# Chunk attention into a phase MLP: token mix with tokens on the output partitions, transposes as four 64x64 tiles, q and k in 512-byte runs, and an order written out

## Chip, cores and metric

The kernel runs on one core of a Trainium2 chip. The metric is the device time of one execution in microseconds (us), the median of several runs. A profile of one execution is read beside it.

## What is computed

The inputs q, k and v are float32 of shape (8, 8, 576, 64): batch, heads, tokens, head size. Attention works inside chunks of 64 tokens; its result x has 576 tokens of 512 channels for each batch element. A phase layer follows, with a mix over all tokens, and a last product with a ReLU.

```python
scores = (q_c @ k_c.T) / 8                 # for every batch element, head and chunk of 64 tokens
x = softmax(scores) @ v_c                  # x: (8, 576, 512), heads side by side
theta = x @ w_theta                        # 512 x 512
zr, zi = x * cos(theta), x * sin(theta)
y = w_tok_r @ zr + w_tok_i @ zi            # 576 x 576 each, over the tokens
u = x + y
out = u + max(u @ w_ch, 0)                 # 512 x 512, float32
```

## The kernel before

Batch elements are taken in four pairs. A pair has 1152 tokens, which make nine tiles of 128 tokens (NT = 9). Tiles 0 to 3 belong to the first element of the pair, tiles 5 to 8 to the second, and the middle tile 4 (MID) holds the last 64 tokens of the first and the first 64 tokens of the second. GROUPS puts the nine tiles into five groups: four of two tiles and the middle tile alone.

Each stage is a function that works on one group or tile of a pair `p`.

- `load_qk` (L108) and `load_v` (L116) load a tile of q, k or v through the GpSimd queue (POOL), which turns float32 into float16. Each read is a run of 64 float32, so 256 bytes. A tile's q and k lie in a buffer of the pool `nat`.
- `a1` (L176) transposes q and k of a group on TensorE (PE) with 128x128 tiles, and VectorE (DVE) copies the result out of PSUM (L183). `a2` (L198) makes the scores, with 64x64 tiles of the array, and ScalarE (ACT) takes the exponential (L205). `a3` (L223) multiplies by v; v has a column of ones, so the sum of the softmax comes with it, and VectorE divides (L230, L231).
- `a4` (L245) transposes x, and ScalarE copies it (L250). `a5` (L261) makes theta with 512-column matmuls, ScalarE takes the cosine and the sine (L271, L275), and VectorE makes zr and zi. In the middle tile, zr of one element and zi of the other are moved to the other half of the partitions by two SyncE (SP) DMAs from a buffer `zmid`, so that one array pass can take both parts of the token sum.
- `tok_w` (L144) transposes the token weights, held in `wnat`. It does this twice, once in the token order of each element of a pair, into `wT[0]` and `wT[1]`.
- `y` (L312) mixes tokens. It puts channels on the output partitions and tokens on the free axis: for each element and each of four channel blocks, nine pairs of 288-column matmuls are summed. VectorE adds x (L320), which gives uT, already transposed for the last product.
- `w` (L332) multiplies a tile of uT by w_ch. With four more matmuls against an identity (L339) it brings u back to token order. ScalarE takes the ReLU (L345), VectorE adds (L347), and SP stores the tile (L349).

PSUM is one pool of four buffers of two banks each; every stage takes its buffer from it. All the loads of the next pair are issued by `load_pair` when a pair starts. The function `weave` mixes two lists of steps, for instance the token mix of pair `p` with the attention of pair `p+1`; the order inside the engines is then set by the tile scheduler. Weight loads stand between those of the first pair: w_theta and the token weights after the middle tile, w_ch at the end.

Of the kernel before, what the change touches and what calls it, by code (L numbers as in the profile page):

```python
# [9 lines left out]
FP32 = mybir.dt.float32  # L10
# [5 lines left out]
def weave(main, filler):  # L16

    n, m = len(main), len(filler)
    done = 0
    for i, step in enumerate(main):  # L20
        step()
        want = ((i + 1) * m) // n
        while done < want:
            filler[done]()
            done += 1
# [3 lines left out]
def kernel(  # L29
# [14 lines left out]
    CH = 64  # L44
# [4 lines left out]
    T = 2 * S  # L49
    NT = T // P  # L50
    HS = S // 2
    KT = S // P
    scale = 1.0 / math.sqrt(D)
    MID = NT // 2


    GROUPS = [(0, 2), (2, 2), (4, 1), (5, 2), (7, 2)]
    VP = D + 2

    const = ctx.enter_context(tc.tile_pool(name="const", bufs=1))  # L60
    glob = ctx.enter_context(tc.tile_pool(name="glob", bufs=1))
    psum = ctx.enter_context(
        tc.tile_pool(name="psum", bufs=4, space=bass.MemoryType.PSUM)
    )
    nat = ctx.enter_context(tc.tile_pool(name="nat", bufs=6))
    qkp = ctx.enter_context(tc.tile_pool(name="qkp", bufs=3))
    epool = ctx.enter_context(tc.tile_pool(name="epool", bufs=6))
    pairp = ctx.enter_context(tc.tile_pool(name="pairp", bufs=2))
    trig = ctx.enter_context(tc.tile_pool(name="trig", bufs=3))
    outp = ctx.enter_context(tc.tile_pool(name="outp", bufs=4))  # L70


    id16 = const.tile([P, P], FP16, name="id16")
    make_identity(nc, id16)
    pihalf = const.tile([P, 1], FP32, name="pihalf")
    nc.vector.memset(pihalf, math.pi / 2.0)

    wtheta16 = glob.tile([P, NDB, DM], FP16, name="wtheta16")
    wch16 = glob.tile([P, NDB, DM], FP16, name="wch16")


    wT = [glob.tile([P, 2 * KT + 1, S], FP16, name=f"wT{i}") for i in range(2)]
    wnat = glob.tile([P, KT + 1, 2, S], FP16, name="wnat")
    NV = 2 * NT
    v16 = glob.tile([P, NV, H, VP], FP16, name="v16")
    nc.gpsimd.memset(v16[:, :, :, D : D + 1], 1.0)

    def psum2(name, dtype=FP32):
        n = 1024 if dtype == FP32 else 2048
        return psum.tile([P, n], dtype, name=name, tag="ps")  # L90

# [3 lines left out]
    def tok_ranges(j):  # L95

        if j < MID:
            return [(0, 0, j * P, P)]
        if j > MID:
            return [(0, 1, j * P - S, P)]  # L100
        return [(0, 0, MID * P, CH), (CH, 1, 0, CH)]

    def load_qk(p, j):
        t = nat.tile([P, 2, H, D], FP16, name="qk16")
        nats[p, j] = t
        for ti, ap in enumerate((q, k)):
            for pp, bb, s0, n in tok_ranges(j):
                nc.gpsimd.dma_start(  # L108
                    t[pp : pp + n, ti],
                    ap[2 * p + bb, :, s0 : s0 + n, :].rearrange("h s d -> s h d"),  # L110
                )

    def load_v(p, j):
        slot = (p % 2) * NT + j
        for pp, bb, s0, n in tok_ranges(j):
            nc.gpsimd.dma_start(  # L116
                v16[pp : pp + n, slot, :, 0:D],
                v[2 * p + bb, :, s0 : s0 + n, :].rearrange("h s d -> s h d"),
            )

    def load_tok_w():
        for ri, ap in enumerate((moe_w_tok_r, moe_w_tok_i)):
            nc.gpsimd.dma_start(
                wnat[:, 0:KT, ri, :],
                ap[0 : KT * P, :].rearrange("(a p) s -> p a s", p=P),
            )
            nc.gpsimd.dma_start(wnat[0:CH, KT, ri, :], ap[KT * P : S, :])
# [5 lines left out]
    def tok_w(par, kt):  # L133
        ps = psum2("ps_wT", FP16)
        for tb in range(KT + 1):
            nt = P if tb < KT else CH
            if kt < 2 * KT:
                s0 = (kt % KT) * P + (CH if par else 0)
                parts = [(slice(0, P), kt // KT, s0)]
            else:  # L140
                s0 = 0 if par else KT * P
                parts = [(slice(ri * CH, ri * CH + CH), ri, s0) for ri in range(2)]
            for rows, ri, s0 in parts:
                nc.tensor.transpose(  # L144
                    ps[rows, tb * P : tb * P + nt],
                    wnat[0:nt, tb, ri, s0 : s0 + rows.stop - rows.start],
                    id16[0:nt, 0:nt],
                )
        if kt % 2:
            nc.vector.tensor_copy(out=wT[par][:, kt, :], in_=ps[:, 0:S])  # L150
        else:
            nc.scalar.copy(out=wT[par][:, kt, :], in_=ps[:, 0:S])


    st = {}

    def new_pair(p):
        st[p] = dict(
            x=pairp.tile([P, NT, DM], FP16, name="x16", bufs=1),
            xT=pairp.tile([P, NDB, T], FP16, name="xT"),  # L160
            zr=pairp.tile([P, NT, DM], FP16, name="zr16"),
            zi=pairp.tile([P, NT, DM], FP16, name="zi16"),
            qkT={},
            eT={},
        )

    def a1(p, g):

        j0, n = GROUPS[g]
        ps = psum2("ps_qkT", FP16)  # L170
        psv = ps.rearrange("p (w e s) -> p w e s", w=2, e=NE)
        for jj in range(n):
            t = nats.pop((p, j0 + jj))
            for w in range(2):
                for e in range(NE):
                    nc.tensor.transpose(  # L176
                        psv[:, w, e, jj * P : jj * P + P],
                        t[:, w, 2 * e : 2 * e + 2, :].rearrange("s h d -> s (h d)"),
                        id16,
                    )  # L180
        qkT = qkp.tile([P, 2, NE, 2 * P], FP16, name="qkT")
        st[p]["qkT"][g] = qkT
        nc.vector.tensor_copy(  # L183
            out=qkT[:, :, :, 0 : n * P], in_=psv[:, :, :, 0 : n * P]
        )

    def a2(p, g):

        j0, n = GROUPS[g]
        qkT = st[p]["qkT"].pop(g)  # L190
        ps = psum2("ps_sT")
        psv = ps.rearrange("p (r j e c) -> p r j e c", r=2, j=2, e=NE)
        for jj in range(n):
            for e in range(NE):
                for par in range(2):
                    for cp in range(2):
                        sl = slice(jj * P + cp * CH, jj * P + cp * CH + CH)
                        nc.tensor.matmul(  # L198
                            psv[cp * CH : cp * CH + CH, par, jj, e, :],
                            qkT[par * D : par * D + D, 1, e, sl],  # L200
                            qkT[par * D : par * D + D, 0, e, sl],
                        )
        eT = epool.tile([P, 2, NE, 2, CH], FP16, name="eT")
        st[p]["eT"][g] = eT
        nc.scalar.activation(  # L205
            out=eT[:, 0:n].rearrange("p j e r c -> p r (j e) c"),
            in_=psv[:, :, 0:n].rearrange("p r j e c -> p r (j e) c"),
            func=AF.Exp,
            scale=scale,
        )  # L210

    def a3(p, j, g):

        j0, n = GROUPS[g]
        eT = st[p]["eT"][g]
        slot = (p % 2) * NT + j
        ps = psum2("ps_x")
        psv = ps.rearrange("p (f c) -> p f c", f=2)
        for h in range(H):
            hf, h4 = h // NE, h % NE  # L220
            for cp in range(2):
                sl = slice(cp * CH, cp * CH + CH)
                nc.tensor.matmul(  # L223
                    psv[sl, hf, h4 * (D + 1) : (h4 + 1) * (D + 1)],
                    eT[sl, j - j0, h // 2, h % 2, :],
                    v16[sl, slot, h, 0 : D + 1],
                )
        px = psv[:, :, 0 : NE * (D + 1)].rearrange("p f (h c) -> p f h c", h=NE)
        recip = trig.tile([P, 2, NE, 1], FP32, name="recip")
        nc.vector.reciprocal(out=recip, in_=px[:, :, :, D : D + 1])  # L230
        nc.vector.tensor_tensor(  # L231
            out=st[p]["x"][:, j, :].rearrange("s (f h d) -> s f h d", f=2, h=NE),
            in0=px[:, :, :, 0:D],
            in1=recip.broadcast_to((P, 2, NE, D)),
            op=ALU.mult,
        )

    def a4(p, g):

        j0, n = GROUPS[g]  # L240
        ps = psum2("ps_xT", FP16)
        psv = ps[:, 0 : NDB * n * P].rearrange("p (a s) -> p a s", a=NDB)
        for jj in range(n):
            for db in range(NDB):
                nc.tensor.transpose(  # L245
                    psv[:, db, jj * P : jj * P + P],
                    st[p]["x"][:, j0 + jj, db * P : db * P + P],
                    id16,
                )
        nc.scalar.copy(  # L250
            out=st[p]["xT"][:, :, j0 * P : (j0 + n) * P], in_=psv
        )

    def a5(p, g):

        j0, n = GROUPS[g]
        ps = psum2("ps_theta")
# [94 lines left out]
    def c(f, *a):  # L352
        return lambda: f(*a)
# [100 lines left out]
```

The softmax here doesn't subtract the row's maximum and nothing guards it: scores larger than these inputs give would overflow.

## Time and profile before

| | |
|---|---|
| median of 3 runs | 245.84 us (244.75 to 246.86) |
| profiled execution, first to last instruction | 243.4 us; this span is the only time of it that the page gives |
| PE busy | 208.7 us (86%) |
| DVE, ACT, POOL busy | 129.1, 111.2, 105.9 us |
| DMA queue q0 (POOL's loads) | 114784 packets, 16.54 MB |
| DMA queue q1 (SP's stores and moves) | 5888 packets, 9.96 MB |
| one store of a tile to landing | 2.1 us (median) |

PE is TensorE's matmuls, whose ends are modelled and overlap, so its busy time is an upper bound of its work. A name like `ps_y` is the tile that an instruction writes, and L312 is line 312 of the kernel. The page counts a DMA's bytes where they land, so the float32 loads count half of what they read.

### The profile page before, as it was taken

The numbers are of one execution on the slowest core, as the hardware profiler recorded it, in microseconds if no ns is written. First come the engines' busy times: TensorE is split into PE (matmuls) and PEld (weight loads), VectorE is DVE, ScalarE is ACT, GpSimd is POOL, SyncE is SP. The second block draws the span as 40 slices with busy tenths as digits, with TensorE's granted clock in tenths as the row PEclk, the third lists the DMA queues.
The fourth block names the chain that finished last, engine by engine and source line by source line (L and its number), as shares of the span: only waits on it lengthen the run. The fifth ranks groups of instructions, "written<-read, shape, count | busy, mean of one in ns | idle before, by whom it ended". The sixth has DMA issues, their size and how long they took to land.

```text
span 243.4 us, 6143 instructions
## 1 busy us (share of the span) xinstructions
PE 208.7 (86%) x2692; PEld 143.6 (59%) x2692; DVE 129.1 (53%) x217; ACT 111.2 (46%) x136; POOL 105.9 (44%) x133
## 2 busy tenths in 40 slices
PE   0453799289999979899998998999989989999992
PEld 0232566156578856456876764658867645577761
DVE  0223327424457466686754637868447377653353
ACT  2012289134862257688414283884132738810132
POOL 9997497869928997220998000008000000000000
PEclk9999999758999999999999999999999999999999
DMA  7999999999999999993999511439901213400226
GB/s 47 145 135 168 185 155 176 166 140 103 148 87 59 149 146 186 211 143 110 81 149 143 89 66 43 131 109 66 69 3 47 86 41 94 148 3 0 89 88 215
DMA packets 120698, 26.89 MB, mean 110 GB/s; under 512 B 113376, under 2 KB 116064, under 8 KB 120672
## 3 DMA queue, kind: packets, MB, share of 16 engines
q0 software_dynamic: 114784, 16.54, 99.1%
q1 hardware_dynamic: 5888, 9.96, 11.8%
q8 instruction: 21, 0.34, 0.6%
q14 instruction: 5, 0.04, 0.0%
HBM read 33.06 MB, written 9.44 MB: 175 GB/s over the span
## 4 chain that ended last, share of the span: by engine, by line
PE 71%; DVE 8%; POOL 7%; DMA 6%; ACT 5%; issue 1%; POOLq 0%; DVEq 0%
PE ps_y L312 30%; PE ps_uw L332 11%; PE ps_theta L261 11%; PE ps_qkT L176 5%; POOL qk L108 4%; DMA wnat<-in_moe_w_tok_r_dram 4%; PE ps_x L223 3%; PE ps_xT L245 3%; PE ps_wT L144 3%; PE ps_uw L339 3%; DMA zr<-zmid 2%; POOL v L116 2%; PE ps_sT L198 2%; DVE x L231 2%; ACT cos L271 2%; DVE qkT L183 2%
## 5 line engine op out<-in xcount | busy, mean ns | idle before, releaser
L108 POOL DMA_DIRECT2D qk<-in_q_dram x40 | 35.8, 904 | 54.2 <-PE ps_qkT L176 49.0
L320 DVE TENSOR_TENSOR uT<-ps_y,xT 128x576 f16<-128x576 f32 x32 | 24.2, 757 | 46.7 <-PE ps_y L312 46.7
L312 PE MATMUL ps_y<-wT,zr 128*128 128x288 f16 x288 | 44.4, 293 | 4.2 <-DMA zr<-zmid 4.0
L332 PE MATMUL ps_uw<-wch,uT 128*128 128x512 f16 x144 | 42.6, 380 | 3.2 <-DVE x L231 2.3
L345 ACT ACTIVATE relu<-ps_uw 128x512 f32<-128x512 f32 x36 | 21.5, 598 | 46.4 <-PE ps_uw L339 46.2
L205 ACT ACTIVATE eT<-ps_sT 128x1024 f16<-128x1024 f32 (+1 forms) x20 | 18.4, 938 | 50.7 <-PE ps_sT L198 50.7
L312 PE MATMUL ps_y<-wT,zi 128*128 128x288 f16 x288 | 41.5, 290 | 0.0
L116 POOL DMA_DIRECT2D v<-in_v_dram x40 | 34.3, 895 | 7.6 <-PE ps_x L223 7.1
L108 POOL DMA_DIRECT2D qk<-in_k_dram x40 | 35.8, 909 | 2.4 <-DMA wnat<-in_moe_w_tok_r_dram 1.8
L312 PEld LDWEIGHTS <-zr 128*128 128x128 f16 x288 | 26.9, 99 | 12.9 <-DMA zr<-zmid 4.2
L261 PE MATMUL ps_theta<-wtheta,xT 128*128 128x512 f16 x144 | 33.7, 379 | 0.5 <-DVE o L347 0.5
L312 PEld LDWEIGHTS <-zi 128*128 128x128 f16 x288 | 28.6, 99 | 7.7
L176 PE MATMUL ps_qkT<-id,qk 128*128 128x128 f16 x288 | 22.1, 231 | 11.5 <-DMA qk<-in_q_dram 9.7
L339 PE MATMUL ps_uw<-id,uT 128*128 128x128 f16 x144 | 31.5, 219 | 0.0
L183 DVE COPY qkT<-ps_qkT 128x2048 f16<-128x2048 f16 (+1 forms) x20 | 22.0, 1114 | 17.1 <-PE ps_qkT L176 16.1
L347 DVE TENSOR_TENSOR o<-ps_uw,relu 128x512 f32<-128x512 f32 x36 | 24.7, 688 | 10.7 <-ACT relu L345 10.5
L176 PEld LDWEIGHTS <-qk 128*128 128x128 f16 x288 | 18.1, 102 | 14.0 <-DMA qk<-in_q_dram 10.6
L332 PEld LDWEIGHTS <-uT 128*128 128x128 f16 x144 | 14.0, 97 | 17.9 <-DVE x L231 3.5
L231 DVE TENSOR_TENSOR x<-ps_x,recip 128x512 f16<-128x512 f32 x36 | 24.2, 688 | 0.7
L271 ACT ACTIVATE cos<-ps_theta,pihalf 128x1024 f16<-128x1024 f32 (+1 forms) x20 | 20.7, 1034 | 7.7 <-PE ps_theta L261 7.5
L250 ACT COPY xT<-ps_xT 128x1024 f16<-128x1024 f16 (+1 forms) x20 | 18.6, 928 | 12.3 <-PE ps_xT L245 12.3
L261 PEld LDWEIGHTS <-xT 128*128 128x128 f16 x144 | 13.4, 98 | 14.9 <-issue 0.8
(35 smaller groups left out, 181.0 us busy)
## 6 DMA issues: line engine op xcount, KB each, us to landing
out_dram<-o SPq DMA_DIRECT2D x32, 256.0 KB, 2.1
qk<-in_q_dram POOLq DMA_DIRECT2D x32, 128.0 KB, 5.2
qk<-in_k_dram POOLq DMA_DIRECT2D x32, 128.0 KB, 5.6
v<-in_v_dram POOLq DMA_DIRECT2D x32, 128.0 KB, 4.9
out_dram<-o SPq DMA_DIRECT2D x8, 128.0 KB, 3.1
wnat<-in_moe_w_tok_r_dram POOLq DMA_DIRECT2D x1, 576.0 KB, 9.1
wnat<-in_moe_w_tok_i_dram POOLq DMA_DIRECT2D x1, 576.0 KB, 11.0
qk<-in_q_dram POOLq DMA_DIRECT2D x8, 64.0 KB, 5.3
```

Source lines behind the costliest of these rows:

```text
L108: nc.gpsimd.dma_start(t[pp : pp + n, ti], ap[2 * p + bb, :, s0 : s0 + n, :].rearrange("h s d -> s h d"),)
L116: nc.gpsimd.dma_start(v16[pp : pp + n, slot, :, 0:D], v[2 * p + bb, :, s0 : s0 + n, :].rearrange("h s d -> s h d"),)
L176: nc.tensor.transpose(psv[:, w, e, jj * P : jj * P + P], t[:, w, 2 * e : 2 * e + 2, :].rearrange("s h d -> s (h d)"), id16,)
L183: nc.vector.tensor_copy(out=qkT[:, :, :, 0 : n * P], in_=psv[:, :, :, 0 : n * P])
L231: nc.vector.tensor_tensor(out=st[p]["x"][:, j, :].rearrange("s (f h d) -> s f h d", f=2, h=NE), in0=px[:, :, :, 0:D], in1=recip.broadcast_ ...
L261: nc.tensor.matmul(ps[:, jj * DM : jj * DM + DM], st[p]["xT"][:, db, j * P : j * P + P], wtheta16[:, db, :], start=(db == 0), stop=(db == ...
L271: nc.scalar.activation(out=cos[:, 0:n].rearrange("p a e -> p (a e)"), in_=pin, func=AF.Sin, bias=pihalf, scale=1.0,)
L312: nc.tensor.matmul(psv[:, hf, 0:HS], z[:, j, db * P : db * P + P], wT[bb][:, kt, hf * HS : hf * HS + HS], start=(i == 0), stop=(i == 2 * KT),)
L320: nc.vector.tensor_tensor(out=s["uT"][:, db, sl].rearrange("p (f c) -> p f c", f=2), in0=psv[:, :, 0:HS], in1=s["xT"][:, db, sl].rearrange ...
L332: nc.tensor.matmul(ps[:, 0:DM], uT[:, db, j * P : j * P + P], wch16[:, db, :], start=(db == 0), stop=(db == NDB - 1),)
L339: nc.tensor.matmul(ps[:, DM + db * P : DM + db * P + P], uT[:, db, j * P : j * P + P], id16,)
L347: nc.vector.tensor_tensor(out=o, in0=ps[:, DM : 2 * DM], in1=r, op=ALU.add)
```

## The change

The order of all work is now a written list, `ORDER`, which a loop at the end walks through; the tile scheduler takes it as it is. A step is a letter for the stage, the pair, the group or tile, and for TensorE steps the PSUM slot: `T.0A.0` transposes q and k of group A of pair 0 into wide slot 0. PSUM is three wide slots of two banks and two thin slots of one bank, and each step names its own.

Groups are now M (the middle tile) and A, B, C and D, of 256 tokens each. In a group of two tiles, a partition takes two consecutive tokens of q and k with one read of 512 bytes, so a partition holds an even and an odd token; copies after the transposes and the exponential put the tokens back in order. v is still loaded tile by tile with 256-byte reads. A tile of x then consists of two runs of 64 tokens that are 128 tokens apart, and the columns of the one `wT` that is left stand in the same order.

The transposes of q, k, x and the token weights, and the product with v, are cut into 64x64 tiles, four to a wave; the two halves of the rows write different PSUM banks. The token mix `y` has tokens on the output partitions: for a tile, nine 512-column matmuls, with `wT` stationary and z moving; for the middle tile, nine pairs of matmuls of 64 output partitions. u is then transposed back (`u_t`, `u_copy`), which takes the place of the identity matmuls. The ReLU and the last addition are one VectorE instruction. Each tile is stored with one DMA, whose rows in DRAM are two runs of 64. In the middle tile the token sum begins with the part that comes from `zmid`.

```diff
+ORDER = """
+q.0A new.10 q.0B v.0B init.00 k.0A q.0C q.0M k.0B new.00 v.0A k.0M T.0A.0 tk.0A lt.00
+tq.0A S.0A.1 e.0A v.0M T.0B.2 tk.0B V1.0A.0 lw.00 tq.0B v1.0A V0.0A.1 v0.0A S.0B.2 k.0C
+T.0M.0 lw.01 X.0A.1 tq.0M e.0B tk.0M q.1B S.0M.2 x.0A e.0M V1.0B.0 H.0A.1 V0.0M.2 v0.0M
+g.0A v1.0B V1.0M.2 V0.0B.0 v1.0M X.0M.2 x.0M v0.0B X.0B.0 q.0D v.0C q.1M TW.00.1 x.0B
+H.0M.2 z.0A twd.00 H.0B.0 g.0M k.0D z.0M g.0B T.0C.2 lc.00 twa.00 tq.0C TW.01.0 z.0B
+TW.02.1 v.0D twd.01 tk.0C twa.02 S.0C.2 twd.02 twa.01 Y.00.0 Y.01.1 e.0C V1.0C.0 v.1M
...
+Y.36.1 w.34 W.35.0 y.36 w.35 Y.37.1 y.37 U.36.0 U.37.1 u.36 u.37 W.36.0 Y.38.1 w.36
+W.37.0 y.38 w.37 U.38.1 u.38 W.38.0 w.38
+""".split()
...
+    GROUPS = {
+        "M": (MID, None, KT * P),
+        "A": (0, 0, 0),
+        "B": (2, 0, GT),
+        "C": (5, 1, 0),
+        "D": (7, 1, GT),
+    }
...
+    nat = ctx.enter_context(tc.tile_pool(name="nat", bufs=8))
...
+    outp = ctx.enter_context(tc.tile_pool(name="outp", bufs=4))
...
+        nc.gpsimd.dma_start(
+            t.rearrange("p h s d -> p h (s d)"),
+            ap[2 * p + bb, :, s0 : s0 + GT, :].rearrange(
+                "h (p s) d -> p h (s d)", s=2
+            ),
+        )
...
+    def qk_t(p, g, slot):
...
+        for w in range(2):
+            for e in range(NE):
+                for s in range(n):
+                    for r in range(2):
+                        for h in range(2):
+                            nc.tensor.transpose(
+                                psv[half[h], r, e, w, s, :],
+                                t[half[r], w, 2 * e + h, s, :],
+                                id16[half[r], half[r]],
+                            )
...
+    def attn(p, g, f, slot_ps):
...
+        for h4 in range(NE):
+            h = f * NE + h4
+            for r in range(2):
+                for cc in range(n):
+                    rows, to = (half[cc], cc) if n == 2 else (half[r], 0)
+                    nc.tensor.matmul(
+                        psv[half[r], to, h4, :],
+                        eT[rows, h % 2, r if n == 2 else 0, h // 2, :],
+                        v16[rows, slot + (r if n == 2 else 0), h, 0 : D + 1],
+                    )
...
+    def y(p, j, slot):
+        s = st[p]
+        ps = psum1("ps_y", slot)
+
+        if j == MID:
+            parts = [(half[bb], slice(KT * P, S), bb) for bb in range(2)]
+        else:
+            bb = int(j > MID)
+            jl = j - bb * (MID + 1)
+            parts = [(slice(0, P), slice(jl * P, jl * P + P), bb)]
+        for i in range(2 * KT + 1):
+            for rows, cols, bb in parts:
+                if i == 0:
+                    z, jz, kt = s["zi"] if bb else s["zr"], MID, 2 * KT
+                else:
+                    kt = i - 1
+                    z = s["zr"] if kt < KT else s["zi"]
+                    jz = bb * (MID + 1) + kt % KT
+                nc.tensor.matmul(
+                    ps[rows], wT[:, kt, cols], z[:, jz, :],
+                    start=(i == 0), stop=(i == 2 * KT),
+                )
...
+    def add_x(p, j):
...
+    def u_t(p, j, slot):
...
+    def u_copy(p, j):
...
+        if j % 2:
+            nc.vector.tensor_copy(out=uT, in_=psv)
+        else:
+            nc.scalar.copy(out=uT, in_=psv)
...
-        r = outp.tile([P, DM], FP32, name="relu", bufs=3)
-        nc.scalar.activation(out=r, in_=ps[:, 0:DM], func=AF.Relu)
+    def relu_add(p, j):
+        u = st[p].pop(("u", j))
         o = outp.tile([P, DM], FP32, name="o32")
-        nc.vector.tensor_tensor(out=o, in0=ps[:, DM : 2 * DM], in1=r, op=ALU.add)
-        for pp, bb, s0, n in tok_ranges(j):
-            nc.sync.dma_start(out[2 * p + bb, s0 : s0 + n, :], o[pp : pp + n])
+        nc.vector.scalar_tensor_tensor(
+            out=o, in0=st[p].pop(("ps_uw", j)), scalar=0.0, in1=u, op0=ALU.max, op1=ALU.add
+        )
+        if j == MID:
+            to = out[2 * p : 2 * p + 2, KT * P : S, :]
+        else:
+            bb = int(j > MID)
+            jl = j - bb * (MID + 1)
+            s0 = (jl // 2) * GT
+            to = out[2 * p + bb, s0 : s0 + GT, :].rearrange(
+                "(r c t) d -> c r t d", r=2, t=CH
+            )[jl % 2]
+        nc.sync.dma_start(to, o)
...
+    with tc.manual_schedule():
+        for step in ORDER:
+            kind, at, *slot = step.split(".")
+            g = int(at[1]) if at[1].isdigit() else at[1]
+            work[kind](int(at[0]), g, *map(int, slot))
```

The letters of the stages: q, k, v, lt, lc and lw load; T, tq and tk are the transposes of q and k and their copies; S and e the scores and exponentials; V0, V1, v0 and v1 the product with v and its division, for half the heads each; X and x the transpose of x and its copy; H, g and z theta, cosine and sine, and zr and zi; TW, twd and twa the token weights; Y and y the token mix and the addition of x; U and u the transpose of u and its copy; W and w the last product, and the ReLU, addition and store.

## The prediction

> **What bounds the kernel now.** I read the page first, then the windows view over one pair's stage, then the chain of waits inside that stage and at the start, and last the DMA view of two short windows.
>
> ```profile
> span 243.4 us, 6143 instructions
> ## 1 busy us (share of the span) xinstructions
> PE 208.7 (86%) x2692; PEld 143.6 (59%) x2692; DVE 129.1 (53%) x217; ACT 111.2 (46%) x136; POOL 105.9 (44%) x133
> ...
> q0 software_dynamic: 114784, 16.54, 99.1%
> q1 hardware_dynamic: 5888, 9.96, 11.8%
> ...
> HBM read 33.06 MB, written 9.44 MB: 175 GB/s over the span
> ```
>
> TensorE is the bound: VectorE and ScalarE are busy half the time. Two like stages, one pair each, show it in the windows view:
>
> ```profile
> 113.00:162.00 49.00, 47.26 (x649) 32.81 (x646) 30.90 (x53) 25.25 (x32) 16.73 (x20) 1.00 0.92 101
> 162.00:211.70 49.70, 47.97 (x652) 33.23 (x651) 31.61 (x53) 25.96 (x32) 5.26 (x6) 1.00 0.40 68
> ```
>
> The first columns are length and PE busy. Prices come from the chain of waits (start, length, instruction, count):
>
> ```profile
> 113.06 2.21 PE ps_y L312 x18
> 115.26 1.79 PE ps_qkT L176 x32
> 117.05 2.21 PE ps_y L312 x18
> 119.25 0.37 PE ps_sT L198 x32
> ...
> 120.56 2.31 PE ps_y L312 x18
> ...
> 123.76 0.25 PE ps_sT L198 x16
> ```
>
> A 288-column matmul costs 2.21/18 = 0.123 us, a 128x128 transpose 1.79/32 = 0.056, and a 64x64 matmul (0.37-0.25)/16 = 0.008, since four run at once. The y after ps_sT takes 2.31, not 2.21: a change of array shape costs 0.1. A 512-column matmul costs 0.216 (ps_theta, 16 in 3.45); ps_x, only two tiles at once, 0.016 (32 in 0.63, 16 in 0.37). One pair sums to 144x0.123 + 72x0.216 + 144x0.056 + 144x0.008 + 144x0.016 = 44.8, with 22 shape changes 46.9 of 49.0 us. So 4% is stall.
>
> The start is the other loss. Before the first ps_y at 48.4 the chain runs:
>
> ```profile
> 16.95 9.06 DMA wnat<-in_moe_w_tok_r_dram
> ...
> 42.48 5.87 DMA zr<-zmid
> 48.35 0.05 issue
> 48.40 0.66 PE ps_y L312 x2
> ```
>
> Token weights, then a ScalarE run of sines, then the shift of the middle tile behind other traffic.
>
> The DMA view of a window that holds one lone store, and of one full of wide loads:
>
> ```profile
> q1 hardware_dynamic: 144, 0.26, 34.1%
> out_dram<-o SPq DMA_DIRECT2D x1, 256.0 KB, 2.0
> ```
> ```profile
> DMA packets 1434, 1.57 MB, mean 196 GB/s; under 512 B 54, under 2 KB 1433, under 8 KB 1433
> ```
>
> The first window is 2.0 us: the store took 0.341x16x2.0 = 10.9 us of engine time, 0.68 on each of 16, which is 24 GB/s an engine. The loads land 196 GB/s in fp16, so they read 392 in fp32: 24.5 GB/s an engine, the same limit. Stores cost nothing today because 16 engines share them.
>
> [...] 2048-byte store packets take 84 ns alone and 96 beside loads (medians), one 256-byte read more each.[...]
>
> **The change, part by part.**
>
> *Stores.* This decides. L349 writes 128 rows in a row; the new store writes a tile whose rows are two runs of 64, `(r c t) d -> c r t d`, and the built instruction indeed carries 2x64 rows on the DRAM side, 128 partitions on the other; the middle tile too.[...] The 10.9 us of engine time of one store then take 5.46 us instead of 0.68, and 36 stores 196.5. PE's work from the first store to the end is 148 us (below), so stores become the bound. Four o32 buffers let four be outstanding; then w waits on VectorE, with the y, u and z behind it in the fixed order, thin PSUM stays full, and PE stops. The shifts of the middle tile use the same queue and wait behind up to four stores.[...] By 50 us I expect 7.5 of the 16.54 MB landed (34 us at 175 GB/s, slice rates of before, then slower as buffers fill); 9.0 MB land later, 18 MB read, 1.1 MB on each engine, 46 us at 24.5. The two bounds on this term are 0 (hidden) and 46 (strictly in turn). The 84 to 96 speaks for in turn; but prefetch may run further ahead, so I take 33.
>
> *Token mix.* 144 matmuls of 288 become 72 of 512, 15.6 us, plus the middle tile's 9 pairs on two column halves: 1.9 if a pair runs at once, 3.9 if not. Half-width transposes of wnat today start 2 to 4 ns apart in pairs, so 1.9. Sum 17.5 against 17.7: no change. The 36 identity matmuls that added u become 36 transposes at the same 2.0, and ScalarE's Relu and VectorE's add (598 and 688 ns, x36) become one VectorE pass near 688 and a copy of uT, shared between the two engines. Both stay near their old totals, under 0.7 of any stage, beside PE.
>
> *Quarter tiles.* q, k: 4.0 to 288x0.008 = 2.3; xT: 2.0 to 1.2; ps_x on four tiles: 2.3 to 1.2. A pair falls from 44.8 to 41.0. Array shape changes fall from 117 to 73 in the program. From the first Y to the end, the order holds 161.6 us of PE, changes included; 13.9 of it comes before the first store, w.01. PSUM is now three wide and two narrow slots, each waiting for its own evacuation; the stall of before was 4%, and I take 5% (0 to 10 as bounds: 162 to 180 us).
>
> *Loads.* 80 requests for q and k become 48, most with 512-byte reads; v keeps 40. POOL issues about 0.9 us each, off the path after the start.
>
> *Order and start.* wT is built once, and attention no longer stands behind wnat on PE. 4.3 MB go out up to the second token weight, which lands near 27.5 at 175 GB/s. theta lands near 18; H.0A at half clock (the first transposes run 0.105 apart) ends at 21.7; ScalarE then does table 1.3, sines 2.1, two xT copies 1.6, and the sines of M and B, to 33; three weight copies at 0.8 and a k copy at 1.0 bring the first Y to 36 instead of 48.4. First store: 36+14 = 50.
>
> **The sum,** on the span: 50 + 196.5 + 33 + 2 for the last landing (median 2.1) = 281.5. The runs' median lies 2.4 above the span of 243.4, so 284.
>
> **Rivals.** *Stores spread over 16 engines after all* (faster). Then PE bounds: 36 + 161.6/0.95 + 3 for the tail = 209, with 2.4 about 212. For it: everything the 16-engine trace shows.[...] It wins once a store's time on its engines falls under 161.6/36 = 4.5 us, so from four engines (2.7) up.
>
> *Two engines, loads hidden.* 50+196.5+2+2.4 = 251. For it: much can be prefetched. Against: the byte rate is the same for both.
>
> *Small instructions limit PE.*[...] Around 77.4 us 144 instructions start in 1.18 us[...].[...] Beside the store limit PE has the room.
>
> **How the numbers follow.** Two engines with loads in turn 0.57, two engines with loads hidden 0.25; spread and PE-bound 0.13; spread with slow feed 0.05. The forecast is the first, 284. From 236 to 304 the range holds the first two (low end: first store at 45, packets and loads a little better; high end: 46 for loads and 10 of idle queue) and most of the last. A change of 1% is about what a measurement of this kernel can tell. Faster: 0.13 and a little of the last, 0.14; within 1% 0.03; slower 0.83.
>
> **What would show it.** Right: stores that land in over 6 us, up to 25, median several times 2.1; q1's share of all 16 engines' time still near 11.8x243/282 = 10% although two of them are full; PE idle waiting for VectorE, VectorE for a store; the middle shift landing late; load landings far above 5 us. A ps_qkT of 64 quarters near 0.5 to 0.6 us and the first ps_y near 36 would confirm the cheaper front. Wrong: stores still landing in about 2 us; then the time should be near 212.

## The result, and the profile after

| | before | after |
|---|---|---|
| median | 245.89 us (4 runs) | 300.54 us (4 runs, 299.77 to 302.86) |
| ratio, 95% interval | | 1.2238 (1.2175 to 1.2301) |
| profiled execution, span | 243.4 us | 298.3 us (time of that execution 300.1) |

The kernel became slower by 54.7 us. The forecast was 284.0, with a range of 236 to 304. Medians and ranges in this document count every execution, while a ratio leaves out those over 1.5% above the fastest of the same kernel (three of six in wide_x, for instance), so a ratio need not be the quotient of two medians.

The page of the changed kernel, with the lines that answer to those of before, the two rows of a queue (packets, MB, share of 16 engines) and two groups of ScalarE:

```profile
span 298.3 us, 8370 instructions
## 1 busy us (share of the span) xinstructions
PE 197.9 (66%) x3834; PEld 102.9 (34%) x3834; DVE 126.4 (42%) x248; ACT 133.1 (45%) x137; POOL 77.5 (26%) x100
...
GB/s 87 169 193 193 181 170 164 166 82 123 125 63 79 64 71 77 168 159 80 86 67 94 53 63 56 54 53 55 53 66 55 51 51 51 53 51 52 51 51 40
...
q0 software_dynamic: 81504, 16.54, 64.2%
q1 hardware_dynamic: 5320, 9.96, 9.4%
...
DMA 44%; PE 28%; ACT 9%; POOL 4%; issue 4%; DVE 3%; DVEq 0%; ACTq 0%; POOLq 0%
...
L259 ACT COPY kT<-ps_qkT 128x1024 f16<-128x1024 f16 x16 | 20.8, 1302 | 32.6 <-PE ps_qkT L241 27.8
...
L296 ACT ACTIVATE eT<-ps_sT 128x1024 f16<-128x1024 f32 x16 | 21.0, 1310 | 6.6 <-PE ps_sT L283 6.5
```

No engine is the bound any more: TensorE fell from 86% of the span to 66%, and 44% of the chain that ended last is DMA. q1, the queue of the stores, has only 9.4% of the time of 16 engines. That looks like a queue with room, as 11.8% did before. The flat end of the GB/s row says what it is: for some 100 us the whole core moves 51 to 56 GB/s in all slices but one (66). A DMA view of ten of those us, in which nothing but stores is moving:

```profile
DMA packets 254, 0.51 MB, mean 51 GB/s; under 512 B 4, under 2 KB 4, under 8 KB 254
...
q1 hardware_dynamic: 254, 0.51, 13.1%
```

13.1% of 16 engines is 2.1 engines. One store of 0.262 MB at 51 GB/s takes 5.1 us. So a store moves at the rate of two engines, both full, and the share of 16 hides it. The 4 packets under 512 B in this view, for two stores, say the same: in the kernel before, 16 such packets come with each store.

Where the span went is read best from the packets of the stores. The first begins at 65.2 us and the last at 296.7. Between them the queue is idle for 28.9 us (13.7 from 111.6, 3.1 from 139.1, 12.1 from 149.4), and moves for 202.6, which is 5.6 us per store. With 1.6 for the end, 65.2 + 28.9 + 202.6 + 1.6 = 298.3. The windows view (length, busy PE, PEld, DVE, ACT and POOL, then granted clock, DMA share, GB/s) shows three kinds of stage:

```profile
100.00:120.00 20.00, 5.54 (x50) 2.47 (x51) 1.06 (x2) 0.00 (x0) 7.74 (x10) 0.53 0.72 79
240.00:260.00 20.00, 16.64 (x86) 7.24 (x86) 8.09 (x13) 1.17 (x2) 0.00 (x0) 0.91 0.13 52
280.00:298.30 18.30, 0.00 (x0) 0.00 (x0) 0.00 (x0) 0.00 (x0) 0.00 (x0) 0.50 0.12 47
```

In the first, the engines mostly stand still: TensorE is busy for 5.5 of 20 us. In the second, TensorE is busy for 16.6 us, most of it with 512-column matmuls, but finishes only four tiles: one in 5 us, which is the pace of the stores. In the last all work is done, and stores drain for 17 us. Between the first and the second, from 160 to 240, TensorE is busy for 77.4 of 80 us, and from 161.5 us on the stores move beside it without a pause. The chain of waits names what stands behind the first and the second (start, length, what):

```profile
41.60 6.67 PE ps_y L435 x18
...
49.53 1.94 PE ps_y L435 x9
...
72.29 42.13 DMA qk<-in_k_dram
...
119.03 12.41 DMA qk<-in_k_dram
...
131.72 21.84 DMA qk<-in_k_dram
...
224.35 16.41 DMA out_dram<-o
...
242.83 33.82 DMA out_dram<-o x2
```

From 72 to 154 the path is loads of k, but for about 5 us; from 224 on it is mostly stores. One load of k took 42 us. The DMA view of part of that time, in which another load of k is issued, shows why:

```profile
DMA  1111111111111499938799711111111951111111
GB/s 43 44 39 44 39 44 39 44 39 44 39 44 39 66 130 123 105 48 98 104 196 186 117 39 44 39 43 44 39 43 42 131 69 39 52 35 39 44 35 43
...
q0 software_dynamic: 2680, 0.45, 29.4%
q1 hardware_dynamic: 384, 0.77, 11.4%
...
qk<-in_k_dram POOLq DMA_DIRECT2D x1, 256.0 KB, 29.4
```

For most of these 20 us the DMA engines are busy to 0.1, two of sixteen, and move 39 to 44 GB/s, less than stores alone. The packets take turns one for one: from 80 to 86 us, 117 packets of loads and 117 of stores move. A load is spread over all sixteen, as the short stretches at 0.9 show. The reading that fits is that fourteen engines then have nothing left to do, and that the load's parts on the two engines of the stores take turns with these. (The trace does not number the engines.) The load of k issued in this window has landed only when those parts have: 29.4 us after its issue. The waits of after (total, times, longest) say who pays:

```profile
PE ps_qkT L241 <- DMA qk<-in_k_dram: 27.9, 4, 20.8
...
DVE o L480 <- DMA out_dram<-o: 20.2, 6, 4.4
```

### The profile page after: what moved, and what is told of

Its sections match the earlier page's. It is cut to its first block, busy times and chain, and to the rows that moved or that the text cites. A ratio compares the mean times of both kernels' runs of the same rounds, so it can differ in the third digit from the quotient of the medians.

```text
span 298.3 us, 8370 instructions
## 1 busy us (share of the span) xinstructions
PE 197.9 (66%) x3834; PEld 102.9 (34%) x3834; DVE 126.4 (42%) x248; ACT 133.1 (45%) x137; POOL 77.5 (26%) x100
## 3 DMA queue, kind: packets, MB, share of 16 engines
q1 hardware_dynamic: 5320, 9.96, 9.4%
## 4 chain that ended last, share of the span: by engine, by line
DMA 44%; PE 28%; ACT 9%; POOL 4%; issue 4%; DVE 3%; DVEq 0%; ACTq 0%; POOLq 0%
DMA qk<-in_k_dram 27%; DMA out_dram<-o 17%; PE ps_y L435 10%; PE ps_theta L374 7%; PE ps_uw L471 4%; POOL v L179 2%; ACT kT L259 2%; ACT eT L296 2%; ACT cos L390 2%; POOL qk L158 2%; ACT sin L394 2%; PE ps_uT L453 1%; PE ps_qkT L241 1%; PE ps_x L316 1%; DVE x L329 1%
## 5 line engine op out<-in xcount | busy, mean ns | idle before, releaser
L435 PE MATMUL ps_y<-zr,wT 128*128 128x512 f16 (+1 forms) x180 | 45.2, 404 | 3.9 <-DVE o L480 2.8
L435 PE MATMUL ps_y<-zi,wT 128*128 128x512 f16 (+1 forms) x180 | 46.9, 395 | 0.0
L435 PEld LDWEIGHTS <-wT 128*128 128x128 f16 (+1 forms) x360 | 32.1, 104 | 42.8 <-issue 11.2
L444 DVE TENSOR_TENSOR u<-ps_y,x 128x512 f16<-128x512 f32 x36 | 24.8, 688 | 52.1 <-PE ps_y L435 51.9
L465 ACT COPY uT<-ps_uT 128x512 f16<-128x512 f16 x20 | 11.8, 588 | 65.8 <-PE ps_uT L453 65.8
L480 DVE SCALAR_TENSOR_TENSOR o<-ps_uw,u 128x512 f32<-128x512 f32 x36 | 24.8, 688 | 32.7 <-DMA out_dram<-o 20.2
L259 ACT COPY kT<-ps_qkT 128x1024 f16<-128x1024 f16 x16 | 20.8, 1302 | 32.6 <-PE ps_qkT L241 27.8
L329 DVE TENSOR_TENSOR x<-ps_x,recip 128x512 f16<-128x512 f32 (+1 forms) x40 | 25.5, 638 | 1.4
L296 ACT ACTIVATE eT<-ps_sT 128x1024 f16<-128x1024 f32 x16 | 21.0, 1310 | 6.6 <-PE ps_sT L283 6.5
L394 ACT ACTIVATE sin<-ps_theta 128x1024 f16<-128x1024 f32 (+1 forms) x20 | 18.7, 934 | 0.0
L158 POOL DMA_DIRECT2D qk<-in_q_dram x16 | 14.5, 908 | 13.6 <-PE ps_qkT L241 8.1
```

What stands on the lines that cost most here:

```text
L259: nc.scalar.copy(out=t.rearrange("p x c t -> p x (c t)").rearrange("p x (i s) -> p x s i", s=2), in_=ps,)
L296: nc.scalar.activation(out=eT.rearrange("p h r e (i s) -> p (h r e) s i", s=2), in_=ps.rearrange("p (x s i) -> p x s i", s=2, i=CH // 2), ...
L329: nc.vector.tensor_tensor(out=st[p]["x"][:, j0 : j0 + n, f * NE * D : (f + 1) * NE * D].rearrange("p c (h d) -> p c h d", h=NE), in0=psv[: ...
L394: nc.scalar.activation(out=sin[:, 0:n].rearrange("p a e -> p (a e)"), in_=pin, func=AF.Sin)
L435: nc.tensor.matmul(ps[rows], wT[:, kt, cols], z[:, jz, :], start=(i == 0), stop=(i == 2 * KT),)
L444: nc.vector.tensor_tensor(out=u, in0=st[p].pop(("ps_y", j)), in1=st[p]["x"][:, j], op=ALU.add)
```

## The experiments

**One store as two DMAs.** Everything of the change stays; each store is issued as two DMAs of 64 rows, so the DRAM side carries 64 rows and no outer two.

```diff
-        nc.sync.dma_start(to, o)
+        for r in range(2):
+            nc.sync.dma_start(to[r], o[half[r]])
```

> The changed kernel, with each tile stored by two DMAs of 64 rows in a row, in place of one DMA of two runs of 64. Theory (the store's outermost dimension of 2 puts it on two DMA engines, and these two bound the kernel): stores land in about 2 to 3 us again, PE is the bound, 41.6 (the first Y of the changed kernel) + 161.6/0.95 + 3 + about 2 outside the span = 217 us. Rival (the written order, the quarter tiles or the loads cost the time, and late stores only follow from it): 295 to 305 us.

Measured: 236.85 us (236.08 to 238.14), ratio to before 0.9635 (0.9585 to 0.9685). Page, then chain:

```profile
span 234.4 us, 8424 instructions
...
PE 192.2 (82%) x3834; PEld 101.5 (43%) x3834; DVE 126.4 (54%) x248; ACT 132.9 (57%) x137; POOL 77.5 (33%) x100
...
PE 55%; ACT 21%; issue 8%; DVE 8%; DMA 5%; POOL 2%; SPq 0%; ACTq 0%; POOLq 0%
...
out_dram<-o SPq DMA_DIRECT2D x72, 128.0 KB, 2.4
```
```profile
93.94 6.14 DMA zr<-zmid
...
100.14 4.06 PE ps_y L435 x18
...
107.10 0.95 PE ps_qkT L241 x108
108.06 5.09 issue
113.14 0.48 PE ps_qkT L241 x13
```

This one edit takes back 63.7 us, more than the whole loss: with its stores spread, the change is a gain of 3.65%. The two traces also show where the time was lost. From its 4789th to its 7343rd instruction TensorE takes 67.2 us in the changed kernel (from 162.9) and 67.3 here (from 131.2), so nothing is lost there: of the 63.9 us between the spans, 31.7 lie before this stretch, where loads came late, and 32.2 after it, where stores drain.

But 236.85 is not the 217 that the theory named for a PE bound. The chain shows two places: a wait of 6.1 us for the shift of the middle tile, and a stop of 5.1 us inside a run of 64x64 transposes for which the trace shows no wait.

**The same bytes, dimensions in another order.** Is it the number of DMAs, or the outer dimension? Here a store stays one DMA with the same addresses; only the order of the two DRAM dimensions is turned, 64x2 for 2x64.

```diff
-            to = out[2 * p : 2 * p + 2, KT * P : S, :]
+            to = out[2 * p : 2 * p + 2, KT * P : S, :].rearrange("b t d -> t b d")
...
-                "(r c t) d -> c r t d", r=2, t=CH
+                "(r c t) d -> c t r d", r=2, t=CH
```

> The changed kernel with the same single store to the same two runs of rows, its DRAM dimensions named in the other order: 64 rows outermost, the 2 runs inside. The same addresses are written, but rows stand in other places of the output. Theory (the outermost dimension decides): as with two DMAs, about 217 us, a store landing in 2 to 3 us. Rival (two runs 128 rows apart are slow for the memory, whatever the order of the dimensions): 295 to 305 us.

Measured: 236.92 us, ratio 0.9618 (0.9567 to 0.9669); again not 217, but the same as two_dmas.

```profile
q1 hardware_dynamic: 5824, 9.96, 12.0%
...
out_dram<-o SPq DMA_DIRECT2D x36, 256.0 KB, 2.6
```

A store lands in 2.6 us again. One DMA, as many bytes and the same 2048-byte pieces as the changed kernel: only the order of the DRAM dimensions, and so the size of the outermost, differs, and the 64 us hang on it. The 504 packets on q1 that came on top of the 5320 are of 4 bytes: 16 with each store in place of 2.

**Four runs.** Here a tile's rows are carried as four runs of 32, and the middle tile goes as two DMAs.

```diff
-                "(r c t) d -> c r t d", r=2, t=CH
+                "(r c t) d -> c r t d", r=4, t=CH // 2
```

> The changed kernel with each tile stored as four runs of 32 rows, outermost dimension 4 (the middle tile by two DMAs of 64 rows); rows stand in other places of the output. Theory (outermost 4 gives four engines): a store takes 10.9/4 = 2.7 us of four engines, 32 stores 87 us, under PE's 170, so 217 to 225 us, with a store's packets on four engines and about 100 GB/s while one runs alone. Rival (any outermost dimension under 16 is equally bad, or the number of runs counts): 295 us or more.

Measured: 245.6 us over 20 runs, ratio 0.9975 (0.9954 to 0.9996). Neither number. In a window of which the first part has one store moving, five slices in a row run at 98 to 106 GB/s, so at twice the rate of two engines:

```profile
GB/s 41 0 25 0 8 57 57 74 74 98 106 98 106 106 74 90 66 8 25 0 8 49 66 74 147 123 197 188 197 287 336 180 98 90 82 57 16 8 25 66
```

So with an outermost dimension of 4 a store moves at the rate of four engines, and takes about 2.6 us at that rate. That is far below the 4.5 us in which PE makes a tile, and still 8.7 us are lost against two_dmas. Its chain has the place:

```profile
93.98 18.58 DMA v<-in_v_dram
```

A load of v holds the path for 18.6 us where two_dmas has its 6.1 for the shift. The loads issued from 93 to 98 us land in 18 to 20 us here and in 11 to 13 in two_dmas. So stores on four engines delay the loads that share these, though they are no bound themselves.

**The narrow store alone, in the kernel before.** 32 of the 40 stores of the old kernel get the pattern of two runs of 64; nothing else changes.

```diff
-        for pp, bb, s0, n in tok_ranges(j):
-            nc.sync.dma_start(out[2 * p + bb, s0 : s0 + n, :], o[pp : pp + n])
+        if j == MID:
+            for pp, bb, s0, n in tok_ranges(j):
+                nc.sync.dma_start(out[2 * p + bb, s0 : s0 + n, :], o[pp : pp + n])
+            return
+        bb = int(j > MID)
+        jl = j - bb * (MID + 1)
+        s0 = bb * CH + (jl // 2) * 2 * P
+        to = out[2 * p + bb, s0 : s0 + 2 * P, :].rearrange(
+            "(r c t) d -> c r t d", r=2, t=CH
+        )[jl % 2]
+        nc.sync.dma_start(to, o)
```

> The kernel before, with 32 of its 40 stores (all but the middle tile's) written as two runs of 64 rows, as in the changed kernel; rows stand in other places of the output. Theory (this alone makes the loss): first store at 90, 32 stores of 5.46 us = 175, and the 4.7 MB of loads that land after 90 us in the kernel before, 24 us of each engine, in turn: 90+175+24+2+2 = 293 us; 265 to 300. Rival (the loss needs the written order or the four o32 buffers in it): 246 to 255 us.

Measured: 319.59 us, ratio 1.3007 (1.2907 to 1.3107). The direction is the theory's, the size is above its 300. The waits of this kernel:

```profile
PE ps_y L312 <- DMA zr<-zmid: 26.9, 4, 12.8
DVE o L347 <- DMA out_dram<-o: 25.3, 6, 5.9
```

My sum held only the stores and the loads in turn with them. In this kernel the two moves of the middle tile go out on SP's queue behind the stores, and the old order needs them at once: TensorE waits 26.9 us for them, in which no store can be made. The store queue is idle for 17.2 us from 149.0, 13.6 from 210.1 and 5.7 from 267.5. These 36.5 us were not in the sum; the moving itself took less than it had (186 us for 199). In the changed kernel no wait of TensorE for these moves is among the longest; that its order leaves more time before the shifted half is used would explain it, but was not tried.

**No loads after the first pair.** In the changed kernel with its stores, q, k and v are loaded for pair 0 alone.

```diff
+        if p > 0:
+            nats[p, g] = kept[g]
+            return
...
+        if p > 0:
+            return
```

> The changed kernel, stores as changed, but q, k and v of pairs 1 to 3 aren't loaded: those of pair 0 are used again, so the output of those pairs is that of pair 0's tokens. It measures what the loads add to two full DMA engines. Theory (an engine moves store and load bytes in turn): the 6.4 MB that landed after the first store in the changed kernel were 33 us of each engine, and in 29 us the stores stood still while work waited for loads; both go. First store near 62, 36 x 5.46 = 197, the landing and 2 outside: about 262 us. Rival (loads pass beside the stores for nothing, and the store queue alone sets the end): 292 to 301 us.

Measured: 263.82 us (263.38 to 264.15), ratio 1.0745 (1.0708 to 1.0781); span 262.3.

```profile
120.00:220.00 100.00, 94.70 (x1622) 48.93 (x1607) 63.38 (x121) 59.26 (x63) 0.00 (x0) 0.98 0.15 53
```

53 GB/s over 100 us, the store rate, with no load left to wait for. Its store packets begin at 59.4 us and end at 260.8, idle 8.6 of it. The late loads cost 36.0 us of the span, and the difference to after has three parts: 5.8 in the first store (65.2 against 59.4), 20.3 in idle queue (28.9 against 8.6) and 9.8 in moving (202.6 against 192.8). These loads read 12.85 MB after the first store, a sixteenth of which takes 33 us at 24.5 GB/s. So the loads are not hidden: they cost about as much as if loads and stores added up on the two engines. Only 9.8 us of it is slower moving, though. In how much of the idle 20.3 those engines work off loads, and in how much TensorE is short of input, this run does not separate.

**Seven output buffers instead of four.**

```diff
-    outp = ctx.enter_context(tc.tile_pool(name="outp", bufs=4))
+    outp = ctx.enter_context(tc.tile_pool(name="outp", bufs=7))
```

> The changed kernel with seven o32 buffers in place of four, stores as changed. Theory (the two engines' rate is the bound): more buffers only let later work and its loads start earlier, so at most the 29 us in which the stores stood still can go, and the trade with the loads remains: 280 to 300 us. Rival (it is the wait for one of four buffers, on VectorE and then PE in the fixed order, that costs the time): well under 270 us.

Measured: 300.17 us, ratio 1.2227 (1.2186 to 1.2268), just above the theory's 280 to 300; span 298.3 as before the edit. The only wait left at the line that writes `o` is for its matmuls:

```profile
DVE o L480 <- PE ps_uw L471: 14.3, 18, 2.2
```

The 20.2 us that VectorE waited for stores are gone and the time is the same. That wait was the queue's backlog showing, not a shortage of buffers: a queue with 202.6 us to move ends when it ends.

**What was left of the rival's 212.** The next two kernels are two_dmas with one more edit, and the third has both. The first makes the transposes of x with 128x128 tiles again, so the program has 432 fewer matmuls and as many fewer weight loads. It asks whether the stop inside ps_qkT belongs to what is being computed there, or to the place in TensorE's stream of instructions.

```diff
-        psv = ps.rearrange("p (r x) -> p r x", r=2)[:, :, 0 : n * NDB * CH]
...
-                for r in range(2):
-                    for h in range(2):
...
+        psv = ps[:, 0 : n * NDB * P].rearrange("p (a c) -> p a c", c=P)
...
+                nc.tensor.transpose(
+                    psv[:, j * NDB + db, :],
+                    st[p]["x"][:, j0 + j, db * P : db * P + P],
+                    id16,
+                )
```

> The kernel with two DMAs a store, x transposed with 128x128 tiles in place of four 64x64: 144 matmuls in place of 576, 864 PE instructions fewer[...]. Theory A (PE stops because its instruction fetch, 16 KB at a time, comes too late for runs of small tiles; it did so for 12 us in four places): some of the stops go, against 3.4 us more of PE work: 231 to 238 us, with fewer stops. Theory B (fetch doesn't matter, quarter tiles are what they were priced): 3.4/0.95 more, 240 us.

Measured: 231.88 us (228.96 to 234.94), ratio 0.9367 (0.9312 to 0.9422). The run of transposes that had the stop, in the chain:

```profile
104.58 0.62 PE ps_xT L345 x8
105.20 1.20 PE ps_qkT L241 x128
106.40 0.55 PE ps_uT L449 x8
```

128 of the same transposes now run through in 1.20 us. With the stop a second loss goes: after it, two_dmas has a granted clock of 0.5 from 111.5 to 118.3 us, and the eight ps_theta matmuls there take 3.41 us; in wide_x the clock is 1.0 and eight take 1.73. The wait for the shift is gone from this chain, too. The second takes the other place: the part of the token sum that comes from `zmid` goes last, not first.

```diff
-                if i == 0:
+                if i == 2 * KT:
...
-                    kt = i - 1
+                    kt = i
```

> The kernel with two DMAs a store, the token sum taken with the middle tile's part last instead of first. The first Y of pair 1 waited 6.1 us for the shift of the middle tile. Theory (that wait is on the path): eight matmuls of 0.216 can go ahead, so 1.7 us less, 235 us, or up to 1.7 for each of the four pairs, 230. Rival (something else is late at that place, too): 236.5 to 237.5 us.

Measured: 233.57 us (231.77 to 234.1), ratio 0.9497 (0.9458 to 0.9535), so 1.4 points below two_dmas: the wait did cost, but 3.3 us rather than 6.1. The 18 ps_y that stood behind it begin at 98.63 instead of 100.14, and in front of them the chain is now TensorE's own work:

```profile
98.03 0.60 PE ps_sT L283 x48
98.63 3.99 PE ps_y L435 x18
```

The stop in ps_qkT is still there in this kernel (5.14 us at 106.48). Both edits together:

> Two DMAs a store, x transposed with 128x128 tiles, and the middle tile's part of the token sum last. Theory (the stops for instruction fetch and the wait for the middle tile's shift are separate losses): 236.9 - 5.0 - 3.3 = 228.6 us. Rival (both changes free the same stretch around the first Y of pair 1): 231 to 233 us, no better than the 128x128 tiles alone.

Measured: 231.14 us (230.47 to 234.2), ratio 0.941 (0.9381 to 0.9438), the same as wide_x within the intervals. This is the rival's case; the gains do not add: wide_x and combined start the same ps_y at 98.07 and 98.58, so wide_x alone had already freed that stretch. These two are the fastest versions found, 6% below the kernel before.

## Why the forecast was right, and where its sum was off

*The cause.* That a store whose outermost dimension is 2 moves on two engines was my estimate: the stores of before have 128 or 64 rows outermost, and its trace shows no store confined to fewer than sixteen engines. The runs confirm it by turning it both ways: two_dmas and dims_swapped undo it, before_two_runs does it alone. The packets can be counted as well: where stores move, mostly two store packets are in flight at once in the changed kernel, mostly four in four_runs, and up to 16 and more in before and dims_swapped. In these runs an outermost dimension of 2 gave the rate of two engines (51 GB/s), one of 4 that of four (98 to 106), and one of 64 a landing in 2.6 us, near the 2.1 that before has with 128; other sizes were not tried.

*A store at 5.46 us.* It moved at 5.36 without loads (192.8/36) and 5.63 beside them (202.6/36). The 196.5 for all lies between.

*Loads in turn, 33 us.* That loads are not hidden was right, no_late_loads shows it. After the first store it is 35 in after, 28.9 + 202.6 - 196.5, but most of it is not slower moving as I had put it: it is a queue that stands empty, because loads late by 20 to 40 us starve TensorE. What I had kept for the high end as "idle queue" was the larger part of the effect. That the size fits is partly luck: 33 was a value taken between two bounds.

*The start, 36 + 14 = 50.* This term failed. The first ps_y began at 41.6 and the first store packet at 65.2 (issued at 62.8). The 15 us are nearly all of the 16.8 by which the span was short (298.3 against 281.5). Of them the chain of the changed kernel names 6.6 in three stops in which TensorE waited for nothing shown (1.98 at 17.9, 1.96 at 37.6, 2.65 at 52.3), and 2.8 in the first 18 ps_y, which took 0.37 us each and not 0.216. In that stretch the granted clock is 0.5 up to 46.9 us, with ps_y matmuls 0.427 us apart, and 1.0 after it, with 0.216. I had carried the half clock through H.0A and dropped it for Y. 5.8 more belong to late loads by no_late_loads; these parts may overlap.

*VectorE for a store, four buffers.* The wait came as described (20.2 us), but o32_seven shows that it decides nothing.

*The token mix, 17.5 for 17.7.* Nine 512-column matmuls take 1.94 to 2.06, as priced.

*Quarter tiles at 0.008.* 128 in 1.20, 63 in 0.55 and 64 in 0.68 give 0.009 to 0.011. On 1424 such transposes of q, k and x after the first ps_y that is 2 to 4 us, not seen beside the stores.

*ScalarE's copies and exponentials at 1.0.* Where the tokens are put back in order, kT takes 1.302 and eT 1.310; eT was 1.023 in the trace of before. 32 of them make about 10 us more. ScalarE has 21% of the chain of two_dmas.

*The rival of 16 engines, 212.* As a mechanism it is what two_dmas runs, and it was wrong by 25 us in size. The late start and half clock (8.2), the shift (6.1) and stops without a wait after the first ps_y (7.6) are on its chain; wide_x and mid_last give back 5.0 and 3.3 of it by the medians (6.6 and 3.4 by the ratios). Its threshold, "from four engines up", fell too: four_runs gave 245.6. It compared a store's time with PE's time for a tile, and left out that loads share those engines; that the delay of loads cost the 8.7 us is read from the chain of four_runs.

*Small instructions limit PE.* A slow feed as the steady pace was my estimate. In wide_x 128 transposes with their weight loads ran in 1.20 us, 4.7 ns an instruction, where the stretch named for it in before has 8.2 (1.18/144); so that stretch was not at the limit of a feed. A cost of many instructions exists all the same, below.

## What to carry to other kernels

Before a store's access pattern is changed, write down the outermost dimension of its DRAM side: here a split of 128 rows into 2x64 moved the same bytes and cost 64 us, which two DMAs, or the same addresses as 64x2, gave back. (As 64x2 the rows go out in another order, so the tile must be laid out for it; two DMAs need nothing else.) A queue's share of all 16 engines says nothing about the two that it may be using; read the GB/s of a stretch where it moves alone (9.4% and 51 GB/s here). Stores confined to two or four engines slowed the loads that had a part on them (a load of k landed in 29.4 us beside two, loads of v in 18 to 20 beside four), and with four they cost 8.7 us without being the bound.

## What the runs showed that I had not expected

TensorE stops in the middle of runs of small instructions, with no wait for an input in the trace. In two_dmas that is 12.1 us in four stops, 2.08 us from 18.0, 2.01 from 37.5, 2.69 from 52.0 and 5.28 from 107.9, as spacings between two instructions:

```profile
17.62 0.64 PE ps_sT L283 x18
18.26 1.84 issue
20.10 0.27 PE ps_sT L283
...
37.69 1.82 issue
...
52.15 2.50 issue
```

Counted over weight loads and matmuls, these stops come after instruction 446, 1211, 1722 and 4022, and in after, whose times are different, after the same four. The steps between them, 765, 511 and 2300, lie within four of 3, 2 and 9 times 256. The page of two_dmas has a DMA queue of the kind "instruction":

```profile
q8 instruction: 30, 0.49, 0.9%
```

These are 30 packets of 16384 bytes, 0.9 to 1.7 us each, for 7668 weight loads and matmuls: 256 to a packet. In wide_x 26 come with 6804 (262 to a packet), in before 21 with 5384 (256). Their times fit every stop. The four stops of two_dmas end 1.37, 1.48, 1.56 and 1.49 us after the end of the 1st, 4th, 6th and 15th of these packets, so the packets are 3, 2 and 9 apart, as the stops are in blocks of 256. wide_x lost the stop of 5 us and has four others (2.16, 3.10, 1.81 and 1.37 us); they end 1.2 to 1.8 us after its 1st, 4th, 15th and 16th packet. In neither trace does a block of 256 begin sooner than 1.2 us after its packet, and where the packet came early enough there is no stop.

So the stops are read as TensorE waiting for its next 256 instructions, as many as the 128 transposes of wide_x and their weight loads used up in 1.20 us. No run moved the fetches alone. Why a packet comes late is open: the one of the 5.28 us stop took 0.89 us and began 2.9 us after the stop did, while the core moved 173 GB/s. Cutting a transpose into quarters thus has a price in instructions beside its gain in the array: wide_x, with 864 fewer, is 5.0 us faster than two_dmas by the medians.
